# Batch 0 of a chunked-attention and sine-MLP kernel: loads by GpSimd with the cast, units of even and odd blocks, and other places for zeros and key transposes

## The chip, the cores and the metric

The kernel runs on one NeuronCore of a Trainium2 chip. Five engines work on it: TensorE (PE in the profile, with PEld for its weight loads), VectorE (DVE), ScalarE (ACT), GpSimd (POOL) and SyncE (SP, which here only issues DMAs). The metric is the device time of one execution in microseconds, the median of several runs.

## The reference

Two parts follow each other. The attention has 4 batches, 8 heads, 768 positions and 64 elements a head. The positions are cut into chunks of 32; a chunk sees 8 memory rows, and the keys from 16 before it to 8 behind it:

```
for c in range(nc):                      # 24 chunks
    k_full = concatenate([mem_k, k[l_start:r_end]])
    v_full = concatenate([mem_v, v[l_start:r_end]])
    a = softmax(scale * q_c @ k_full.T)
    out[c] = a @ v_full
```

The result, reshaped to 3072 tokens of 512 elements, goes through a feed-forward layer with a hidden width of 2048:

```
h = x @ w_in
s = sin(alpha * h)
g = h + s * s / alpha
out = g @ w_out
```

Inputs and output are float32; the kernel computes in bfloat16 with float32 accumulation.

## The kernel before

A batch's 768 positions are cut into 8 blocks of 96 (three chunks of 32). A block's window is 128 rows: 64 key rows from 16 ahead of the block, 8 memory rows, 56 more key rows. Keys and queries stand transposed in SBUF (`kT`, `qT`: head elements on partitions, two heads to one tile of 128), values stand by window rows (`vw`: 64 elements and a column of ones, which gives the softmax sum). What a chunk may not see is masked: in batch 0 by one more matmul (`mrow` against the indicator `mind`), in the others by a bias of the exponential (`biasm`).

The work is written out by hand as one list of words, `WORDS`, with one line per stage. Each word issues one step, and each engine and each DMA queue executes its steps in the order in which the words issue them. Stage 0 of the list (the first line) is the attention of batch 0; the next three lines hold the feed-forward of one batch beside the attention of the next; the last holds the feed-forward of batch 3. The words that matter here (a digit behind a letter is a head pair, a block or a tile; A, V or P names the engine, ACT, DVE or POOL):

- `dq`, `dk`, `V`: issue loads of q, k and v from POOL's queue, which casts to bfloat16 on the way (L190, L196). `dk068` is k of batch 0, heads 6 and 7.
- `a`: cast a float32 load of q or k to bfloat16 (L683). In the kernel before, head pairs 0 to 2 of batch 0's q and k come as float32 through SP and ACT (L756) and are cast by ACT and DVE.
- `k`, `l`: 12 transposes on PE of a head pair's k or q (L307); `K`, `L`: the copy from PSUM to `kT` or `qT`.
- `s`, `v`: scores with the exponential, and values with the division, of one unit (L347, L372). A unit of batch 0 is a head pair and a half of the blocks: blocks 0 to 3 (half 0) or 4 to 7 (half 1). In the other batches a unit is one block with all heads.
- `t`, `T`: turn a unit's result on PE and copy it to `xT` by DVE or ACT; `c`: the same by a DMA transpose from SP.
- `b`, `h`: feed-forward tile, the first and the second 384 columns (4 matmuls each), `h` followed by the sine on ACT; `q`: the square; `g`: DVE's last step, which fills `gT` and frees the tile's two PSUM banks. Four such pairs of banks exist.
- `o`, `f`: the second matrix product, fed in pieces between the other work; its result goes through one of three `o_sb` buffers to a store on SP.
- `R`, `X`: row loads of k and q of batches 2 and 3 from POOL, and their DMA transposes from SP into `kT` and `qT`.
- `I`, `U`: loads of `w_in` and `w_out` from POOL, by tiles (`I27` is tiles 2 to 6, `I7g` 7 to 15).
- `y`, `z`: matmuls on zeros, 128 or 512 columns each; `C`: constants and zeros; `W`: a table load on ACT.

Loads from POOL are issued by POOL itself, so its queue holds its memsets, copies and load issues in one order.

Of the kernel before, what the change touches and what calls it, by code (L numbers as in the profile page):

```python
# [9 lines left out]
P = 128  # L10
QW = 96
# [15 lines left out]
    ),  # L27
    (
# [5 lines left out]
    ),  # L34
    (
# [5 lines left out]
    ),  # L41
    (
# [5 lines left out]
    ),  # L48
    (
# [72 lines left out]
def kernel(  # L122
# [12 lines left out]
    nc = tc.nc  # L135
# [36 lines left out]
    pts = [consts.tile([P, H * QW + 32], BF, name=f"pt{i}") for i in range(NPT)]  # L172
# [6 lines left out]
    memk_bf = memv_st[0:NK, 0]  # L179
    memk_st = memv_st[96:104].rearrange("n b h d -> n b (h d)")  # L180
    memkT = consts.tile([P, HP, NK], BF, name="memkT")
# [36 lines left out]

    def win(vflat, row, n, height):
        a = vflat[row:row + 1, :]  # L220
        return bass.AP(tensor=a.tensor, offset=a.offset, ap=[[D, height], [QW * D, n], [1, D]])
# [20 lines left out]
    def put_memk(b):  # L242
        nc.vector.tensor_copy(
            kTs[b % 2][:, :, 24:856].rearrange("p g (j c) -> p g j c", c=104)[:, :, :, 40:40 + NM],
            memkT[:, :, NM * b:NM * b + NM].unsqueeze(2).to_broadcast([P, HP, NJ, NM]),
        )
# [289 lines left out]
    class Stage:  # L536
# [39 lines left out]
        def do_P(self, a):  # L576
            self.early(a, 1)
# [311 lines left out]
```

## Time and profile before

| | us |
|---|---|
| median of 3 runs | 215.34 (215.27 to 215.65) |
| profiled execution, its own time | 214.68 |
| span of that execution | 212.8 |
| PE busy | 204.9 (96%) |
| DVE busy | 139.9 (66%) |
| ACT busy | 143.7 (68%) |
| POOL busy | 100.9 (47%) |

The chain of work that ended last is 78% PE, 8% DVE, 5% ACT and 4% DMA; the DMA share is one float32 load of keys at the start (`kq_f<-in_k_dram`). A busy PE is not PE at its peak, since matmuls are pipelined and their ends are modelled; and in the opening PE is also busy with matmuls on zeros, which compute nothing. Times inside the profile count from the start of the span.

### The profile page before, as it was taken

The numbers are of one execution on the slowest core, as the hardware profiler recorded it, in microseconds if no ns is written. First come the engines' busy times: TensorE is split into PE (matmuls) and PEld (weight loads), VectorE is DVE, ScalarE is ACT, GpSimd is POOL, SyncE is SP. The second block draws the span as 40 slices with busy tenths as digits, with TensorE's granted clock in tenths as the row PEclk, the third lists the DMA queues.
The fourth block names the chain that finished last, engine by engine and source line by source line (L and its number), as shares of the span: only waits on it lengthen the run. The fifth ranks groups of instructions, "written<-read, shape, count | busy, mean of one in ns | idle before, by whom it ended". The sixth has DMA issues, their size and how long they took to land.

```text
span 212.8 us, 4568 instructions
## 1 busy us (share of the span) xinstructions
PE 204.9 (96%) x1772; PEld 118.1 (55%) x1772; DVE 139.9 (66%) x210; ACT 143.7 (68%) x229; POOL 100.9 (47%) x142
## 2 busy tenths in 40 slices
PE   7879999999999999999999999999999999999994
PEld 7456665565455556555455555554555555554453
DVE  4788788999452749976766649897247187865010
ACT  2579898978848469968837199887856189891110
POOL 8998605589697297109795048664000022200000
PEclk9999999999999999999999999999999999999999
DMA  5999999999999999999999259999944400000312
GB/s 156 332 158 139 212 207 204 205 139 183 131 160 155 176 114 129 121 144 146 146 152 183 74 125 125 137 157 133 134 104 107 137 0 0 3 2 0 148 52 99
DMA packets 95853, 27.82 MB, mean 131 GB/s; under 512 B 84808, under 2 KB 92376, under 8 KB 95832
## 3 DMA queue, kind: packets, MB, share of 16 engines
q0 software_dynamic: 69152, 13.64, 89.3%
q1 hardware_dynamic: 25720, 12.68, 29.6%
q10 hardware_dynamic: 960, 1.21, 1.7%
q8 instruction: 14, 0.23, 0.6%
q14 instruction: 7, 0.06, 0.1%
HBM read 29.66 MB, written 6.29 MB: 169 GB/s over the span
## 4 chain that ended last, share of the span: by engine, by line
PE 78%; DVE 8%; ACT 5%; DMA 4%; issue 3%; SPq 1%; DVEq 0%; ACTq 0%
PE ps L495 39%; PE ps L457 30%; DMA kq_f<-in_k_dram 4%; PE ps L447 3%; DVE gT L484 2%; PE ps L418 2%; DVE x_blk L387 2%; DVE s L480 2%; ACT s L477 2%; PE ps L399 1%; ACT pt L365 1%; PE ps L312 1%; ACT u L472 1%; DVE q_bf L686 1%; DVE rinv L386 0%
## 5 line engine op out<-in xcount | busy, mean ns | idle before, releaser
L495 PE MATMUL ps<-w_out_sb,gT 128*128 128x512 bf16 (+1 forms) x400 | 89.1, 371 | 0.0
L457 PE MATMUL ps<-xT,w_in_sb 128*128 128x384 bf16 x512 | 85.9, 326 | 0.6 <-DVE gT L484 0.4
L484 DVE SCALAR_TENSOR_TENSOR gT<-s,inv_alpha,ps 128x768 bf16<-128x768 f32 x64 | 63.1, 1012 | 12.3 <-ACT s L477 5.2
L457 PEld LDWEIGHTS <-w_in_sb 128*128 128x128 bf16 x512 | 49.7, 98 | 35.2 <-issue 2.0
L472 ACT ACTIVATE u<-ps,alpha_sb 128x768 f32<-128x768 f32 x64 | 56.6, 894 | 16.9 <-PE ps L457 14.4
L495 PEld LDWEIGHTS <-gT 128*128 128x128 bf16 x400 | 37.1, 98 | 37.1 <-DVE gT L484 0.2
L480 POOL TENSOR_TENSOR s<-u 128x768 f32<-128x768 f32 x11 | 17.2, 1568 | 67.2 <-ACT u L472 56.4
L432 ACT ACTIVATE pt<-ps,biasm 128x256 bf16<-128x256 f32 x72 | 27.1, 488 | 10.5 <-PE ps L418 10.5
L502 DVE COPY o_sb<-ps 128x512 f32<-128x512 f32 (+1 forms) x15 | 10.0, 669 | 27.6 <-PE ps L495 25.7
L480 DVE TENSOR_TENSOR s<-u 128x768 f32<-128x768 f32 x23 | 21.9, 953 | 7.6 <-ACT u L472 7.5
L477 ACT ACTIVATE s<-u 128x768 f32<-128x768 f32 x30 | 25.0, 841 | 0.5
L387 DVE TENSOR_TENSOR x_blk<-ps,rinv 96x512 bf16<-96x512 f32 x32 | 22.0, 687 | 1.1
L502 ACT COPY o_sb<-ps 128x512 f32<-128x512 f32 (+1 forms) x10 | 5.7, 572 | 22.0 <-PE ps L495 22.0
L208 POOL DMA_DIRECT2D vw<-in_v_dram x13 | 12.0, 926 | 6.3 <-PE ps L399 5.4
L386 DVE RECIPROCAL rinv<-ps 96x8 f32<-96x8 f32 x32 | 6.4, 199 | 13.1 <-PE ps L447 12.7
L215 POOL DMA_DIRECT2D vw<-in_v_dram x13 | 13.3, 1024 | 1.6 <-DMA vw<-in_v_dram 1.6
L274 POOL DMA_DIRECT2D kst<-in_k_dram x16 | 13.0, 815 | 1.8 <-DMA vw<-in_v_dram 1.2
L268 POOL DMA_DIRECT2D kst<-in_k_dram x16 | 11.1, 691 | 2.1 <-DMA kst<-in_k_dram 1.0
L281 POOL DMA_DIRECT2D q_bf<-in_q_dram x12 | 10.7, 911 | 0.0
L402 ACT COPY xT<-ps 128x384 bf16<-128x384 bf16 x10 | 5.0, 496 | 8.2 <-PE ps L399 8.2
L447 PEld LDWEIGHTS <-pt 128*128 128x128 bf16 x192 | 8.2, 97 | 4.2 <-ACT pt L432 0.3
L447 PE MATMUL ps<-vw,pt 128*128 128x65 bf16 x192 | 8.9, 193 | 0.0
(83 smaller groups left out, 140.7 us busy)
## 6 DMA issues: line engine op xcount, KB each, us to landing
out_dram<-o_sb SPq DMA_DIRECT2D x23, 256.0 KB, 2.2
q_bf<-in_q_dram POOLq DMA_DIRECT2D x12, 128.0 KB, 7.7
kq_f<-in_k_dram SPq DMA_DIRECT2D x3, 384.0 KB, 6.2
kq_f<-in_q_dram ACTq DMA_DIRECT2D x3, 384.0 KB, 7.9
w_in_sb<-in_moe_w_in_dram POOLq DMA_DIRECT2D x1, 1152.0 KB, 12.9
vw<-in_v_dram POOLq DMA_DIRECT2D x7, 128.0 KB, 7.7
vw<-in_v_dram POOLq DMA_DIRECT2D x8, 112.0 KB, 8.1
kst<-in_k_dram POOLq DMA_DIRECT2D x14, 64.0 KB, 5.5
```

The costliest lines, as they stand in the source:

```text
L215: nc.gpsimd.dma_start(vw[72:128, c0:hi, 0:D], win(vflat, base + QW * c0 + 48, hi - c0, 56))
L274: nc.gpsimd.dma_start(kst[72:72 + n, j, :].rearrange("p (h d) -> p h d", d=D), k[b, :, QW * j + 48:QW * j + 48 + n, :].rearrange("h p d -> ...
L387: nc.vector.tensor_tensor(out=x_blk[:].rearrange("p g e d -> p e g d"), in0=otv[0:QW, :, :, 0:D], in1=rinv[:].unsqueeze(3).to_broadcast([Q ...
L432: nc.scalar.activation(pt[:, 0:H * QW].rearrange("p (g e c) -> p g e c", g=2, e=4)[:, :, :, 32 * m:32 * m + 32], sc[:, :, 0:4 * QW].rearra ...
L447: nc.tensor.matmul(otv[:, e, hp, :], pt[:, QW * i:QW * i + P], vws[b % 2][:, 2 * hp + e, j, 0:D + 1],)
L457: nc.tensor.matmul(t["hT"][:, hf, 0:HALF], w_in_sb[:, kt, P * t["ft"]:P * t["ft"] + P], t["xT"][:, kt, HALF * hf:HALF * hf + HALF], start= ...
L472: nc.scalar.activation(t["u"][:], t["hT"][:, :, 0:HALF], ACTF.Sin, scale=alpha_sb[:, ft:ft + 1])
L477: nc.scalar.activation(s2[:], u[:], ACTF.Square)
L480: e.tensor_tensor(out=s2[:], in0=u[:], in1=u[:], op=ALU.mult)
L484: nc.vector.scalar_tensor_tensor(out=gT[:, ft, :].rearrange("p (e c) -> p e c", e=2), in0=t["s2"][:], scalar=inv_alpha[:, ft:ft + 1], in1= ...
L495: nc.tensor.matmul(o[:, c0:c1], gT[:, ft, P * s:P * s + P], w_out_sb[:, ft, c0:c1], start=(ft == 0), stop=(ft == FT - 1),)
L502: copier(state["engines"][state["o"] % len(state["engines"])])(o_sb[:, c0:c1], o[:, c0:c1])
```

## The change

It changes the first line of words and what it calls, and rewrites the order of the other lines.

1. Loads of batch 0. The float32 loads through SP and ACT and the six casts (`a`) go. All of q, k and v of batch 0 come from POOL's queue with the cast, by head pairs: q 0-1 is issued ahead of the identity, then k 0-1, k 2-3, k 4-5, q 2-3, v 0-1, q 4-5, k 6-7, v 2-3, q 6-7, v 4-5, and v 6-7 in four pieces of even and odd blocks (`G030`, `G031`). The loads of w_in 0 to 1 and 2 to 6 come behind them.
2. Units of batch 0 are the even and the odd blocks of a head pair instead of the first and the last four. Tiles 0 and 1 of batch 0's feed-forward are opened by the new word `j` on even columns, and these two are finished by two DVE instructions of 384 columns instead of one of 768.
3. Memory rows. mem_k is transposed in float32 and copied from PSUM straight to its places in both `kT`; mem_v of batch 0 is spread by head pairs from the float32 load (`n`, three on ACT, one on DVE) instead of a cast and one DVE copy.
4. Zeros and constants. Zeros of `pt`, of the first `kT` and of the first `vw` and its ones move from POOL to DVE, the sums behind `mind` to DVE and its copies to ACT; those of the second `kT` and `vw` stay on POOL and come later. Twelve matmuls on 512 columns of zeros take the place of the 40 on 128 columns at the start.
5. Batch 2. The new words `r` and `x` issue work of the batch after next: sixteen row loads (`r16`) and six key transposes (`x6`) stand in the second line of words; `x6` comes ahead of two stores.

The core of the diff, with the first line of words whole and of the second line the beginning and the end:

```diff
-        'y1 y1 y1 Ci y1 a4A We y1 Cb a1A y1 y2 y1 y1 dq068 Cl y1 Cm y1 Cf z1 z1 eVA z1 eVA a0A Ck m0 Cz z1 '
-        'dk068 Cp V024 z1 z1 V002 z1 a2V V068 z1 z1 Cv l0 z1 a5V z1 L0A k1 k0 z1 k2 l1 K1A V046 K0A a6V L1A '
-        's00 s10 s11 K2V l2 k3 L2V K3A s01 v11 dm l3 L3A v10 s20 v01 s30 v00 s31 v30 s21 v31 z1 T01 v20 T30 '
-        'I02 Cs T00 v21 t10 T20 t31 z1 t11 I27 t21 Ws '
+        'n0A Cb dk002 dk024 Ci Cz dk046 We Cd z1 z1 z1 z1 z1 z1 z1 z1 z1 z1 z1 z1 k0 z1 K0V Cm z1 Cp n1V l0 '
+        'z1 z1 dq024 k1 z1 V002 dq046 Ck K1A y1 L0A Cv l1 z1 s01 dk068 s00 L1V s10 v01 s11 z1 Cy v00 V024 '
+        'dq068 l2 z1 k2 n2A K2A n3A V046 L2V t00 G030 v10 t01 G031 s20 v11 l3 dm k3 L3A K3V s21 T11 v20 I02 '
+        's30 v21 s31 v30 Cs T10 v31 T20 T30 T21 T31 Cl Ws Cw I27 '
...
-        'o8 b0 h0 I7g q0V U69 U12 b1 h1 dq108 q1A b4 h4 b3 g0 h3 b6 g1 dk108 q4V g4 q3A b2 h2 h6 b5 h5 Ufg g3 '
+        'j0 j1 h0 I7g q0V h1 g0 q1V dk108 b4 h4 b3 U01 h3 U56 g1 q4V b6 b2 q3A o8 g4 h2 dq108 h6 g3 U45 U12 '
...
-        'g15 f7 h14 V125 k1 k0 g12 l1 K1V k3 L1V L3A q14V K3A K0A V102 dy f9 g14 s61 f16 m1 s70 s3 f13 v0 f3 '
-        'v6 Z2 c6 f6 v3 f5 s542 T3 f10 T0 v4 f6 v2 f2 v1 c4 c2 f7 v7 f1 T1 f3 v5 Ws T7 f8 t5 '
+        'b14 g15 f5 q12A h14 g12 f1 k1 k3 k0 l1 L3A f5 L1A K1V V102 f1 K3A K0V q14A g14 f3 m1 s61 f16 dy s073 '
+        'f14 v6 f5 v3 r16 Z2 c6 v0 f8 s542 f10 t3 v4 f7 v2 c2 T0 v1 c4 x6 f9 v7 We t1 f5 v5 We T7 f6 t5 '
...
+    def load_v_half(b, hp, half):
+        assert b < B - 1
+        vw = vws[b % 2][:].rearrange("p h j c -> p (h j) c")
+        vflat = v.rearrange("b h s d -> (b h s) d")
+        c0 = 2 * hp * NJ + half
...
+        for c, r0, r1 in ((lo, 0, 64), (c0, 72, 128)):
...
+            nc.gpsimd.dma_start(
+                vw[r0:r1, c:c1:2, 0:D],
...
+    def put_memv_first(hp, eng):
+        copier(eng)(
+            vws[0][64:72, 2 * hp:2 * hp + 2, :, 0:D],
+            memv_f[64:72, 2 * hp:2 * hp + 2].unsqueeze(2).to_broadcast([NM, 2, NJ, D]),
+        )
...
         for i in range(4):
-            j = 4 * half + i
+            j = 2 * i + half
...
+    def every_other(cols, half):
+        return cols.rearrange("p (a e c) -> p e a c", e=2, c=QW)[:, half]
...
     def finish(t, gT):
         ft = t["ft"]
+        if t["split"]:
+            for hf in range(2):
+                nc.vector.scalar_tensor_tensor(
+                    out=every_other(gT[:, ft, :], hf),
...
+        def do_j(self, a):
+            self.tile[int(a)] = opened(int(a), self.xT if self.i >= 0 else self.next_x(), True)
+            half_tile(self.tile[int(a)], 0)
...
+        def do_r(self, a):
+            for _ in range(int(a)):
+                self.next_rows()["R"].pop(0)()
+
+        def do_x(self, a):
+            for _ in range(int(a)):
+                self.next_rows()["X"].pop(0)()
...
-    for hp in range(HP - 1):
-        load_f(nc.sync, k, hp, kq_f[hp])
-        load_f(nc.scalar, q, hp, kq_f[4 + hp])
-        if hp == 0:
-            nc.sync.dma_start(memv_f[64:72], mem_v[0].rearrange("h n d -> n h d"))
+    nc.sync.dma_start(memv_f[64:72], mem_v[0].rearrange("h n d -> n h d"))
     nc.vector.memset(zeros[:], 0.0)
     nc.vector.memset(tiny[:], 0.0)
+    nc.vector.memset(ident[:], 0.0)
+    load_one(q, q_bf, 0, 0, 2)
+    masks.make_identity(nc, ident[:], nomemset=True)
     nc.vector.memset(mcol[:], 0.0)
-    masks.make_identity(nc, ident[:])
-    for vw in vws:
-        nc.gpsimd.memset(vw[0:32, 0, 0, 0:D], 0.0)
-        nc.gpsimd.memset(vw[96:128, H - 1, NJ - 1, 0:D], 0.0)
+    nc.vector.memset(vws[0][0:32, 0, 0, 0:D], 0.0)
...
     def const_k():
-        nc.vector.tensor_copy(memk_bf, memk_f[0:NK])
...
+                mt[:, g, :], memk_f[0:NK, 2 * g:2 * g + 2, :].rearrange("p e d -> p (e d)"),
+                ident_f[0:NK, 0:NK]
...
     def const_v():
-        for vw in vws:
-            nc.gpsimd.memset(vw[:, :, :, D:D + 1], 1.0)
+        nc.vector.memset(vws[0][:, :, :, D:D + 1], 1.0)
+
+    def const_w():
+        nc.gpsimd.memset(vws[1][:, :, :, D:D + 1], 1.0)
+        nc.gpsimd.memset(vws[1][96:128, H - 1, NJ - 1, 0:D], 0.0)
```

More of the change, by code (lines that the diff above doesn't have):

```diff
@@ L171 @@
     NPT = 8
-    pts = [consts.tile([P, H * QW + 32], BF, name=f"pt{i}") for i in range(NPT)]
+    pt_all = consts.tile([P, NPT, H * QW + 32], BF, name="pt")
+    pts = [pt_all[:, i] for i in range(NPT)]
     memv_st = consts.tile([P, B, H, D], BF, name="memv_st")
@@ L462, in half_tile, with opened @@
             )
-    def opened(ft, xT):
+    def opened(ft, xT, split=False):
         hT, bs = banks.pair()
-        return {"ft": ft, "xT": xT, "hT": hT, "bs": bs, "from": [0, 0]}
+        return {"ft": ft, "xT": xT, "hT": hT, "bs": bs, "from": [0, 0], "split": split}
     def sine(t):
@@ L532 @@
     feed = Feed()
+    ahead = {}
     kq = (k_bf, q_bf)
@@ L550, in __init__ @@
             if 1 <= i + 1 < B:
-                self.queue = {"R": row_loads(i + 1), "X": crosses(i + 1)}
+                self.queue = ahead.pop(i + 1, None) or self.row_work(i + 1)
         def next_x(self):
@@ L675, in do_m, with do_n, do_G @@
             put_memv(int(a))
+        def do_n(self, a):
+            put_memv_first(int(a[0]), a[1])
+        def do_G(self, a):
+            load_v_half(*(int(c) for c in a))
         def do_H(self, a):
@@ L725, in do_y, with row_work, next_rows @@
                 nc.tensor.matmul(ps[:, b, c:c + P], zeros[:, 0:P], zeros[:, c:c + P])
+        def row_work(self, b):
+            return {"R": row_loads(b), "X": crosses(b)}
+        def next_rows(self):
+            b = self.b + 1
+            if b not in ahead:
+                ahead[b] = self.row_work(b)
+            return ahead[b]
+        def do_r(self, a):
[4 more added lines that the diff above has]
+                self.next_rows()["X"].pop(0)()
         def do_R(self, a):
@@ L738, in warm @@
         nc.scalar.activation(tiny[:], zeros[0:1, 0:1], func)
-    kq_f = [mlp.tile([P, 2, 6 * D], F32, name="kq_f", tag=t) for t in ("u", "s2") * 4]
     memk_f = mlp.tile([P, H, D], F32, name="memk_f", tag="o_sb", bufs=3)
```

91 lines of the change are left out of this document (45 added, 46 removed), and 29 rows, old and new, of the table WORDS.

## The prediction

> **What bounds the kernel now.** I read the table of windows first, then the chain of work that ended last, then the timeline of the opening, the loads with their landing times, and the groups of instructions of two stretches. The windows, cut where the chain changes its nature (columns: stretch, its length, then busy time and count of PE, PEld, DVE, ACT, POOL, granted clock, DMA share, GB/s):
>
> ```profile
> 0.00:24.78 24.78, 20.51 (x340) 15.44 (x341) 19.23 (x49) 16.21 (x24) 22.33 (x52) 1.00 1.68 198
> 24.78:35.41 10.63, 10.57 (x69) 6.26 (x66) 8.35 (x11) 9.13 (x12) 1.98 (x2) 1.00 1.20 207
> 35.41:75.10 39.69, 39.57 (x405) 22.43 (x405) 27.00 (x38) 29.02 (x52) 28.80 (x37) 1.00 1.80 164
> 75.10:209.75 134.65, 134.22 (x964) 73.94 (x962) 85.27 (x113) 89.02 (x144) 47.80 (x53) 1.00 0.98 104
> ```
>
> From 35.41 to 209.75 PE is idle for 0.12 + 0.43 = 0.55 us in all. Nothing that the change reorders there can win more than about half a microsecond. What can be won lies in the first stretch: 24.78 us of batch 0's attention, in which PE's 20.51 busy us are partly matmuls on zeros. The chain (start, length, what), and the opening's timeline (start, length, engine, line, operation, count):
>
> ```profile
> 2.57 8.45 DMA kq_f<-in_k_dram
> ...
> 14.60 2.22 ACT pt L365 x3
> ...
> 24.95 2.62 PE ps L457 x16
> ```
>
> ```profile
> 1.20 4.45 PE L725 MATMUL ps<-zeros 128*128 128x128 bf16 x40 [1.20 <-DVE tiny L762]
> 6.37 0.81 PE L719 MATMUL ps<-zeros 128*128 128x512 bf16 x3
> 6.40 0.83 ACT L686 CAST q_bf<-kq_f 128x768 bf16<-128x768 f32 x1 [1.95 <-DMA kq_f<-in_q_dram]
> 9.69 0.53 PE L312 MATMUL ps<-ident,q_bf 128*64 128x128 bf16 x12
> 11.25 1.50 ACT L323 COPY kT<-ps 128x768 bf16<-128x768 bf16 x2 [0.20 <-PE ps L312]
> 18.82 2.41 ACT L365 ACTIVATE pt<-ps 128x768 bf16<-128x768 f32 x3
> 22.14 1.48 ACT L402 COPY xT<-ps 128x384 bf16<-128x384 bf16 x3
> 24.64 1.28 ACT L738 ACT_TABLE_LOAD   x1
> 24.78 17.40 PE L457 MATMUL ps<-xT,w_in_sb 128*128 128x384 bf16 x104
> 26.28 0.90 ACT L472 ACTIVATE u<-ps,alpha_sb 128x768 f32<-128x768 f32 x1
> ```
>
> The reader is to see three dates: the third float load of keys lands at 11.02 (2.57 + 8.45), the first exponentials start at 14.60, the first feed-forward matmul at 24.78. From there the chain is PE, with one stretch in which ACT and DVE lead.
>
> **The change part by part.** *Start of the exponentials.* The six float loads and their six casts go; the same data comes through GpSimd's queue, cast on the way. The rows of that queue (KB, us from issue to landing; then two issues on POOL):
>
> ```profile
> q_bf<-in_q_dram POOLq DMA_DIRECT2D x1, 192.0 KB, 7.8
> k_bf<-in_k_dram POOLq DMA_DIRECT2D x1, 192.0 KB, 7.7
> vw<-in_v_dram POOLq DMA_DIRECT2D x1, 64.0 KB, 2.6
> w_in_sb<-in_moe_w_in_dram POOLq DMA_DIRECT2D x1, 640.0 KB, 8.1
> q_bf<-in_q_dram POOLq DMA_DIRECT2D x1, 768.0 KB, 16.5
> k_bf<-in_k_dram POOLq DMA_DIRECT2D x1, 768.0 KB, 19.5
> 21.25 0.89 POOL L191 DMA_DIRECT2D q_bf<-in_q_dram  x1 [0.78 <-ACT pt L365]
> 22.13 0.89 POOL L191 DMA_DIRECT2D k_bf<-in_k_dram  x1
> ```
>
> The last two land at 37.75 and 41.63, so the queue delivers 768 KB in 3.9 us, 198 KB a us. A pair of heads (192 KB) costs 1.0 us once data flows. The time to the first data is the open price: 2.6 us for 64 KB on an idle queue, or 7.7 us for 192 KB beside the float loads. I take the low end, 2.6 + 128/198 = 3.3 us, because the float traffic that stood beside the 7.7 is what the change removes, and I keep 7.7 for the range. The first load is issued at about 0.75 and the second, keys of heads 0 and 1, at about 2.0; that one lands at 5.3. PE cannot use it yet: its twelve matmuls on zeros are 6144 columns, of which the first 5120 cost 4.45 us from 1.20 and the last two 0.27 each, to 6.2. Then come three turns of 0.53, four more zeros and a small transpose of about 0.25 each: 6.2 + 1.6 + 1.25 = 9.1. ACT copies keys and queries (0.75 each back to back, the first 0.8) to 10.65, and the first exponential starts at about 11.0 against 14.60: 3.6 us earlier. In this sum the load has 0.9 us of cover; beyond that each microsecond costs one.
>
> The Trainium skill, page "DMA: Bandwidth & Descriptors", section on the anatomy of a SWDGE DMA, gives a fixed 2.0 us plus bytes over 436 GB/s, an estimate of 2.9 us for this pair. By that the second load lands at 4.9 and the start stays at 11.0; by the 7.7 row it would be 14.5.
>
> *From the first exponential to the last copy into xT, on ACT.* Before, from 14.60 to the table load at 24.64, 10.0 us. After, in the written order: 8 exponentials at 0.77 (6.2, mean of the two rows of three), a key and a query copy (1.5), two of the new spreads of mem_v (n2, n3), each 1024 elements on 8 partitions, 1.05 by the cast row's 0.83 for 768, and six xT copies at 0.49 (2.95): 12.75, to 23.75. Six xT copies where there were four, and the two spreads, are most of the difference. DVE is not later: eight pairs of
>
> ```profile
> L387 DVE TENSOR_TENSOR x_blk<-ps,rinv 96x512 bf16<-96x512 f32 x8 | 5.5, 687 | 0.3
> L386 DVE RECIPROCAL rinv<-ps 96x8 f32<-96x8 f32 x8 | 1.6, 198 | 0.4 <-PE ps L377 0.4
> ```
>
> are 7.1 us and about 2.5 of copies stand between them, from 12.2 to 21.8. Units of even and odd blocks change no count of matmuls. They let the two new opening words (j0, j1) run on even columns while ACT still copies the last two odd ones, so PE starts 1.0 before ACT ends, at about 22.7 instead of 24.78: 2.1 us.
>
> *What is given back at once.* The sine's table load waits for ACT: 23.75 + 1.28 + 0.2 = 25.2, so the first sine gains only 26.28 - 25.2 = 1.1. In 24.78 to 35.41 ACT is busy 9.13 and DVE 8.35 of 10.63 us; the chain there runs over them. Two further costs fall on DVE: square 1 moves to it and the two split tiles are finished in two halves.
>
> ```profile
> L480 DVE TENSOR_TENSOR s<-u 128x768 f32<-128x768 f32 x3 | 2.9, 954 | 1.8 <-ACT u L472 1.8
> ```
>
> That is 0.95 plus perhaps 0.15 a split tile, 1.25 in all; ACT loses 0.85. Of the 2.1 us I take 1.2 as what arrives at the PE-bound part: the sine's 1.1 is the low bound if ACT and DVE lead throughout, 2.1 the high one if they never do.
>
> *GpSimd's queue, and w_in behind it.* Feed-forward tile 4 is the third and needs w_in 2 to 6, issued last. Issue times on POOL, and one issue that met a DVE copy:
>
> ```profile
> L191 POOL DMA_DIRECT2D k_bf<-in_k_dram x2 | 1.6, 812 | 0.0
> L208 POOL DMA_DIRECT2D vw<-in_v_dram x4 | 3.6, 907 | 0.0
> L847 POOL MEMSET kst<- 32x512 bf16 x1 | 0.6, 564 | 0.0
> L844 POOL MEMSET vw<- 128x64 bf16 x2 | 1.0, 804 | 0.0
> 73.33 0.69 POOL L208 DMA_DIRECT2D vw<-in_v_dram  x1 [5.38 <-PE ps L399]
> 9.19 1.83 POOL L215 DMA_DIRECT2D vw<-in_v_dram  x1
> 9.36 1.22 DVE L224 COPY vw<-memv_st 8x4096 bf16<-8x4096 bf16 x1
> ```
>
> From 0.75: eight pair loads at 0.81 (6.5), six V pieces at 0.91 (5.4), four half pieces at 0.69 (2.8), three small ones at 0.7 (2.1), the memsets left on POOL (2.3), identity 0.3: its issue is at about 20.2. It lands 2.6 + 576/198 = 5.5 later at best, 8.1 by its own row: 25.7 to 28.3. PE wants it after 16 matmuls of 17.40/104 = 0.167, at 22.7 + 2.7 = 25.4. I take 25.7, nearest to the idle queue, since six memsets stand just ahead of it; the 0.3 lies inside the ACT and DVE lead. Before, the same point was 24.78 + 2.7 = 27.5.
>
> *At nothing:* the mem_k transposes in float, the zeros and mind moved to DVE and ACT (both wait for loads until about 6), the removed 1.22 copy. If that cover goes, they cost up to 1 us. *Batch 2:* the sixteen row loads keep their place on POOL; six key transposes move ahead of two stores on SP.
>
> ```profile
> 72.22 3.69 SPq L505 DMA_DIRECT2D out_dram<-o_sb  x2
> 76.09 9.87 SPq L296 DMA_TRANSPOSE kT<-kst  x6
> ```
>
> The stores go some 10 us later, to about 82; the third output buffer is free, and the feed of the next output tiles only begins near 91, so this is hidden. Without that cover it costs PE up to 9.9. The six transposes wait for their row loads, and behind them on SP wait those stores and then the query transposes, which move up by the same six. The later words are reordered with the same counts: 0.3 either way.
>
> Sum: 214.68 for the profiled execution (span 212.8 and 1.9 around it) less 1.2 is 213.5; the median of the three runs, 215.34, stands 0.66 higher, so 214.1.
>
> **The rivals.** *Late first data (slower).* Keys 0 and 1 take 7.7 us as their rows do and land at 9.7, 3.5 after PE is ready. The feed-forward starts at 26.2, net 1.2 - 3.5: 2.3 us slower, 217.6; with a landing at 8.0, 1.8 late, 215.9. It decides from a landing at 7.4 (6.2 + 1.2). For it: every 192 KB row. Against: the float loads beside them, and the 2.6.
>
> *w_in late (slower).* POOL's issues stretch, or the piece takes its 8.1: at 28.3 PE stands 0.8 behind the old kernel's 27.5, 216.1. It decides at 27.5. For it: the issue of 1.83 under a DVE copy of 1.22, against 0.91; two such meetings make 22.0 of 20.2. Against: the DVE copies and casts of that form mostly go. The Trainium skill, page "SBUF — State Buffer", section on the two separate sides, says that DVE in a two-port mode locks GpSimd out of the descriptor ring and that loads from ACT or SP are immune; by it this change moves six loads into the exposed queue. The 1.83 agrees.
>
> *All given back (no change).* ACT and DVE lead from 25 to 35 and the extra 1.25 on DVE eats the sine's 1.1: 215.3.
>
> **How the numbers follow.** Forecast 0.6, of its own 213.1 to 214.9; given back 0.13; late first data 0.16; late w_in 0.11. Nothing under 0.2% (0.43 us) can be told from no change, which gives faster 0.6, same 0.13, slower 0.27. The range runs from 212.9 (2.1 kept and 0.3 from the later words) to 216.2, past the late w_in and a landing at 8.0.
>
> **What would show it.** Right: first exponential near 11, PE on zeros until 6.2 with the keys there before, last xT copy near 23.7 with ACT without gaps, first feed-forward matmul near 22.7, and every later boundary earlier by about the same. Wrong: PE waiting for k_bf or q_bf, PE waiting for w_in after 25, gaps on PE between 25 and 36 that were not there, stores waiting behind the transposes after 75.

## The result, and the profile after

The change made the kernel 1.6% slower. Six runs of the changed kernel have a median of 218.69 us (217.71 to 219.19), six of the kernel before 215.31 (214.7 to 215.65): a ratio of 1.0164, 95% interval 1.0138 to 1.0191. The profiled execution took 219.17 us, its span is 217.4; before, 214.68 and 212.8. The spans differ by 4.6, the medians by 3.4; what follows divides up the 4.6. Of e13, e15, e16 and e18 below, one execution each was over 1.5% above the fastest; it stands in the medians shown and is left out of the ratios.

The windows of the changed kernel, cut at the first feed-forward matmul of each stage (columns as in the prediction):

```profile
0.00:25.80 25.80, 21.19 (x303) 13.14 (x303) 15.29 (x51) 16.73 (x26) 22.94 (x39) 0.93 1.36 134
25.80:77.48 51.68, 50.17 (x469) 28.50 (x469) 34.16 (x50) 38.32 (x63) 30.70 (x38) 1.00 1.57 169
77.48:124.42 46.94, 46.78 (x376) 25.89 (x374) 34.18 (x49) 34.95 (x58) 34.08 (x44) 1.00 1.65 147
124.42:171.75 47.33, 46.19 (x357) 24.95 (x355) 30.03 (x43) 32.92 (x55) 8.82 (x7) 1.00 0.88 115
171.75:217.40 45.65, 42.04 (x241) 23.28 (x239) 23.15 (x25) 20.62 (x26) 7.33 (x5) 0.99 0.13 47
```

The same cuts of the kernel before (its first, to 24.78, is in the prediction):

```profile
24.78:74.94 50.16, 49.98 (x473) 28.60 (x471) 35.35 (x49) 38.01 (x62) 30.62 (x38) 1.00 1.67 174
74.94:121.52 46.58, 46.56 (x377) 25.69 (x374) 33.49 (x48) 32.58 (x57) 27.62 (x36) 1.00 1.59 137
121.52:167.58 46.06, 45.90 (x356) 25.02 (x354) 30.03 (x42) 34.02 (x57) 15.88 (x14) 1.00 1.15 123
167.58:212.80 45.22, 41.91 (x241) 23.32 (x239) 21.75 (x24) 22.92 (x30) 4.46 (x3) 1.00 0.13 47
```

The bill is the difference of the lengths: opening +1.02, stage 0 +1.52, stage 1 +0.36, stage 2 +1.27, last stage +0.43, together 4.60. No stretch gained. In stage 0 PE's busy time grew by 0.19 only, so 1.33 of its 1.52 is idle PE; in stage 2, 0.98 of its 1.27 is idle PE. The last 0.43 lies behind the last copy of an output tile: 2.7 us from its end to the span's end before, 3.1 after.

The opening, on PE and then on ACT:

```profile
6.49 0.53 PE L335 MATMUL ps<-ident,k_bf 128*64 128x128 bf16 x12 [0.87 <-DMA k_bf<-in_k_dram]
...
11.65 0.85 PE L335 MATMUL ps<-ident,q_bf 128*64 128x128 bf16 x12 [1.60 <-DMA q_bf<-in_q_dram]
```

```profile
13.84 2.92 ACT L388 ACTIVATE pt<-ps 128x768 bf16<-128x768 f32 x4 [3.24 <-PE ps L381]
...
26.24 1.28 ACT L796 ACT_TABLE_LOAD   x1
...
27.96 1.70 ACT L500 ACTIVATE u<-ps,alpha_sb 128x768 f32<-128x768 f32 x2 [0.22 <-PE ps L484]
```

The chain of work that ended last has one piece of 6.94 us there, the fifth pair load (queries 2 and 3, issued at 4.67), and the turn behind it:

```profile
4.67 6.94 DMA q_bf<-in_q_dram
11.61 0.04 issue
11.65 0.85 PE ps L335 x12
```

PE's order puts the turn of queries 2 and 3 (l1) ahead of the first scores of heads 0 and 1, whose own loads have long landed. So the first exponential comes at 13.84, not at 11.0. (Other profiles of the same opening wait less here; they are set side by side behind e12.) The turn took 0.85 us where the one at 6.49 took 0.53: PE's clock was at half speed for some 3.4 us.

The early stretch of stage 0, with PE idle for 0.86 and 0.38 us:

```profile
25.80 6.02 PE L484 MATMUL ps<-xT,w_in_sb 128*128 128x384 bf16 x36
32.68 2.12 PE L484 MATMUL ps<-xT,w_in_sb 128*128 128x384 bf16 x12 [0.86 <-DVE gT L514]
35.18 2.76 PE L484 MATMUL ps<-xT,w_in_sb 128*128 128x384 bf16 x16 [0.38 <-DVE gT L522]
```

And the chain over the first of those waits:

```profile
28.89 0.97 DVE s L508
29.91 0.05 issue
29.96 1.14 DVE gT L514 x2
31.11 0.88 DVE s L508
32.01 1.14 DVE gT L514 x2
33.15 0.88 DVE s L508
```

DVE works without a gap from 28.89 on: square, split finish, square, split finish, square. The first eight tiles, 10.63 us before (24.78 to 35.41), take 12.30 (25.80 to 38.10).

The start of stage 2, and what POOL and SP did just before it:

```profile
124.42 1.47 PE L484 MATMUL ps<-xT,w_in_sb 128*128 128x384 bf16 x8
...
126.49 5.37 PE L484 MATMUL ps<-xT,w_in_sb 128*128 128x384 bf16 x32 [0.60 <-DMA xT<-x_blk]
```

```profile
118.26 5.28 POOL L304 DMA_DIRECT2D q_bf<-in_q_dram  x6
```

```profile
121.22 5.14 DMA xT<-x_blk
```

The last row is a piece of the chain: PE, after eight matmuls, needs a block that a DMA transpose is still bringing, 5.14 us after its issue. In the kernel before, the same six query loads stood behind a square on POOL and started 8.70 us later, when the transposes were done, and PE began stage 2 without a wait:

```profile
121.52 13.39 PE L457 MATMUL ps<-xT,w_in_sb 128*128 128x384 bf16 x80
...
125.55 1.46 POOL L480 TENSOR_TENSOR s<-u 128x768 f32<-128x768 f32 x1 [10.65 <-issue]
126.96 5.33 POOL L281 DMA_DIRECT2D q_bf<-in_q_dram  x6
```

### The profile page after: what moved, and what is told of

Its sections match the earlier page's. It is cut to its first block, busy times and chain, and to the rows that moved or that the text cites. A ratio compares the mean times of both kernels' runs of the same rounds, so it can differ in the third digit from the quotient of the medians.

```text
span 217.4 us, 4471 instructions
## 1 busy us (share of the span) xinstructions
PE 206.4 (95%) x1734; PEld 115.8 (53%) x1734; DVE 136.8 (63%) x217; ACT 143.5 (66%) x227; POOL 103.9 (48%) x131
## 4 chain that ended last, share of the span: by engine, by line
PE 68%; DVE 13%; DMA 6%; ACT 5%; issue 5%; POOL 2%; DVEq 0%; POOLq 0%; ACTq 0%
PE ps L533 36%; PE ps L484 23%; DVE gT L522 5%; DVE s L508 4%; DMA q_bf<-in_q_dram 3%; PE ps L444 2%; DMA xT<-x_blk 2%; PE ps L473 2%; ACT u L500 2%; DVE x_blk L410 2%; PE ps L335 1%; DVE gT L514 1%; POOL k_bf L189 1%; ACT qT L355 1%; PE ps L373 1%
## 5 line engine op out<-in xcount | busy, mean ns | idle before, releaser
L484 PE MATMUL ps<-xT,w_in_sb 128*128 128x384 bf16 x512 | 86.9, 326 | 2.9 <-DVE gT L522 1.0
L522 DVE SCALAR_TENSOR_TENSOR gT<-s,inv_alpha,ps 128x768 bf16<-128x768 f32 x62 | 61.0, 1012 | 13.0 <-ACT s L505 7.6
L508 POOL TENSOR_TENSOR s<-u 128x768 f32<-128x768 f32 x12 | 18.9, 1584 | 67.2 <-ACT u L500 67.2
L508 DVE TENSOR_TENSOR s<-u 128x768 f32<-128x768 f32 x24 | 23.1, 961 | 10.4 <-ACT u L500 10.3
L505 ACT ACTIVATE s<-u 128x768 f32<-128x768 f32 x28 | 23.5, 842 | 0.7
L206 POOL DMA_DIRECT2D vw<-in_v_dram x12 | 11.1, 926 | 7.1 <-PE ps L422 7.1
L213 POOL DMA_DIRECT2D vw<-in_v_dram x12 | 11.6, 967 | 0.5 <-DMA k_bf<-in_k_dram 0.5
L278 POOL DMA_DIRECT2D w_out_sb<-in_moe_w_out_dram x10 | 6.4, 651 | 6.2 <-DMA w_in_sb<-in_moe_w_in_dram 6.2
```

The costliest lines, as they stand in the source:

```text
L213: nc.gpsimd.dma_start(vw[72:128, c0:hi, 0:D], win(vflat, base + QW * c0 + 48, hi - c0, 56))
L484: nc.tensor.matmul(h.rearrange("p (a c) -> p a c", c=QW) if t["split"] else h, w_in_sb[:, kt, P * t["ft"]:P * t["ft"] + P], every_other(t[ ...
L505: nc.scalar.activation(s2[:], u[:], ACTF.Square)
L508: e.tensor_tensor(out=s2[:], in0=u[:], in1=u[:], op=ALU.mult)
L522: nc.vector.scalar_tensor_tensor(out=gT[:, ft, :].rearrange("p (e c) -> p e c", e=2), in0=t["s2"][:], scalar=inv_alpha[:, ft:ft + 1], in1= ...
```

## The experiments

Ratios are against the kernel before, run on the same chip in the same job. The medians of the kernel before in the five jobs are 214.51, 214.49, 214.27, 214.73 and 214.47. In the expectations, "the kernel before" and "the changed kernel" are the two given ones.

### Which lines cost: e1 and e2

e1 is the changed kernel with its first line of words and the four later lines of the kernel before. e2 is the converse: the kernel before with its own first line, the new units (even and odd blocks) and the four new later lines.

```
e1: WORDS = (after[0], before[1], before[2], before[3], before[4])
e2: WORDS = (before[0], after[1], after[2], after[3], after[4])
```

> The changed kernel's first line of words (its loads, constants, units, mem spreads) with the old kernel's other four lines. Theory 'opening': the loss is made in the opening, because q of heads 2 and 3, the fifth load, lands at 11.6 and stands in PE's order ahead of the first scores; then this kernel keeps most of it, 2 to 3 us slower than before, 217.3 to 218.3. Rival 'later lines': the opening costs only the 1.0 us by which the first feed-forward matmul is later (25.80 against 24.78), the rest comes from the reordered lines; then 216.0 to 216.5.

> The old kernel's opening (float loads through SP and ACT, casts, its constants) with units of even and odd blocks and the changed kernel's other four lines, j0 and j1 and the row loads and key transposes ahead of the stores among them. Theory 'opening': within 0.5 us of before, 214.8 to 215.8, and first feed-forward matmul near 24.8. Rival 'later lines': 1.5 to 2.5 us slower than before, 216.8 to 217.8, with PE waiting behind DVE in the first eight tiles and for the DMA transposes into xT near 122.

e1: 217.43 us, ratio 1.0113 (1.0050 to 1.0177). e2: 218.79, ratio 1.0188 (1.0119 to 1.0257). Stage by stage, from the timelines (us from one first feed-forward matmul to the next):

| | first feed-forward | stage 0 | stage 1 | stage 2 | last stage |
|---|---|---|---|---|---|
| before | 24.78 | 50.16 | 46.58 | 46.06 | 45.22 |
| after | 25.80 | 51.68 | 46.94 | 47.33 | 45.65 |
| e1 | 26.80 | 50.17 | 46.59 | 46.07 | 45.57 |
| e2 | 24.16 | 51.68 | 47.22 | 47.73 | 46.01 |

The lengths of stages 0 to 2 go with their lines of words, to 0.01 us in e1. So the new lines cost by themselves and not as a result of the opening, and the new opening costs by itself too. The last 0.4 comes with e1 as well, whose last line is the old one; no experiment looked for it. e1's time lies where the theory 'opening' had it, but e2 is slower than both theories said, so both parts cost. The two ratios do not add up to that of the change: e2 meets a second wait for the transposes (1.02 us at the start of stage 2 and 0.60 in the last stage), e1 a worse opening.

### The opening's loads: e3, e4, e12

e3 loads four heads of queries in the first load instead of two; e4 puts the turn of queries 2 and 3 behind the first scores; e12 exchanges two loads.

```
e3: -load_one(q, q_bf, 0, 0, 2)   +load_one(q, q_bf, 0, 0, 4)
    -dk002 dk024 ... dq024         +dk004 ...
e4: -Cv l1 z1 s01 dk068 s00 L1V    +Cv z1 s01 dk068 s00 l1 L1V
e12: -dk046 We ... dq024 k1        +dq024 We ... dk046 k1
```

> The changed kernel with one load of q for heads 0 to 3 and one of k for heads 0 to 3 in place of two each; k 4-5 third. Theory 'fifth load': q and k of heads 0 to 3 are then the first two loads, land by about 8.5, the first exponential starts near 11 instead of 13.84, and the total falls by 1.5 to 2.5 us against the changed kernel, to 216.2 to 217.2. Rival 'the queue delivers some 115 KB a us at this stage, whatever the piece': the second load lands near 9.5 to 10, the first exponential near 12.5, and the total falls by about 1.

> The changed kernel with the turn of q of heads 2 and 3 (l1) moved behind the first two score units in PE's order; loads unchanged. Theory 'fifth load in PE's order': the first exponential starts near 11.3 instead of 13.84, two of the sixteen ACT steps run in the gap, and the total falls by 1 to 1.5 us, to 217.2 to 217.7. Rival 'the load itself': the third exponential still waits for q 2-3 and everything behind it keeps its date; the total falls by less than 0.5.

> The changed kernel with two loads of the opening exchanged: queries 2 and 3 ahead of keys 4 and 5; l1 stays ahead of the first scores. Theory A (192 KB loads land one after another, 1.2 to 2.5 us apart, so a load's place in the queue sets its landing): queries 2 and 3 land near 10.2 instead of 11.6, PE's wait of 1.6 us for them shrinks to 0 to 0.4, the first exponential at 12.2 to 12.8 instead of 13.8. Rival B (what holds the load is something else than its place, such as one slow engine of it): it lands at 11 or later. For the end I expect 0.3 to 1.2 us less by theory A.

e3: 220.55 us, ratio 1.0261 (1.0204 to 1.0319). A longer first load holds the first turn back, PE waits 2.46 us for keys and the first exponential comes at 14.69: not the hoped-for gain. e4: 219.29, ratio 1.0229 (1.0156 to 1.0301). Its opening, on ACT and PE:

```profile
11.87 1.51 ACT L388 ACTIVATE pt<-ps 128x768 bf16<-128x768 f32 x2 [0.43 <-PE ps L381]
...
25.14 1.28 ACT L796 ACT_TABLE_LOAD   x1
```

```profile
13.67 0.35 PE L381 MATMUL ps<-qT,kT 64*128 64x96 bf16 x8 [0.79 <-DVE qT L355]
...
24.70 5.55 PE L484 MATMUL ps<-xT,w_in_sb 128*128 128x384 bf16 x32
```

In these two profiles the exponentials start 2.0 us earlier, and the first feed-forward matmul comes 1.1 earlier than in the changed kernel: no better than 24.78. The total gained nothing. e12: 219.23, ratio 1.0247 (1.0183 to 1.0311). PE no longer waits for queries 2 and 3, but it waited 1.87 us for the first keys, ran at half clock behind that, and the first exponential stayed at 13.80.

How far one profile can be trusted here is seen in the six that have the changed kernel's first line word for word:

| | after | e1 | e5 | e6 | e7 | e16 |
|---|---|---|---|---|---|---|
| PE's wait for queries 2 and 3 | 1.60 | none | 0.34 | 1.24 | none | 0.50 |
| first exponential | 13.84 | 11.96 | 12.24 | 13.45 | 12.09 | 12.33 |
| first feed-forward | 25.80 | 26.80 | 25.74 | 25.95 | 25.23 | 26.82 |

So the long wait for the fifth load is no fixed property of the order: without it (e1, e7) the exponentials start near 12 with l1 where it was, and the feed-forward starts at 26.80 and 25.23, on either side of 25.80. That e4's edit gained the 2.0 us is therefore not shown. With the old first line the feed-forward began at 24.78 and 23.98 (e8), so in the mean the new opening costs 1.7 us (26.06 against 24.38), rather than the 1.02 of one pair of profiles, and differences of less than about a microsecond between single openings say little.

### Stage 0 and stage 2: e5, e6, e7, e16, e8

e5 restores the first eight words of stage 0, e6 one letter of batch 2's line, e7 both; e16 restores the eight words but leaves square 1 on DVE. e8 is the kernel before with the converse of e6's letter.

```
e5:  -j0 j1 h0 I7g q0V h1 g0 q1V    +b0 h0 I7g q0V b1 h1 g0 q1A
e6:  -b1 q5A q3V h1                 +b1 q5A q3P h1
e16: -j0 j1 h0 I7g q0V h1 g0 q1V    +b0 h0 I7g q0V b1 h1 g0 q1V
e8:  -q0V g0 q3P R6                 +q0V g0 q3V R6     (kernel before)
```

> The changed kernel with the first eight words of stage 0's line as they were: both tiles opened whole (b0, b1, no split and no finishing in two halves) and square 1 back on ACT. Theory A (the new start of stage 0 costs the 1.5 us by which the first eight tiles grew from 10.6 to 12.3): the first eight tiles take 10.5 to 11.0 us again, the two waits for gT of 0.86 and 0.38 shrink, the time falls by 1.0 to 1.6 us against the changed kernel. Rival B (the 1.5 is the opening's late end, weights and copies that are not ready, and follows wherever PE starts): the eight tiles stay at 12 us and the time does not move by more than 0.4.

> The changed kernel with one letter of batch 2's line changed: square 3 on GpSimd as before, ahead of the six query loads of R6, instead of on DVE. Theory A (with no square ahead of them the six loads start at 118 instead of 127 us and run beside the transposes into xT, which then take 5.1 us and stop PE at the start of stage 2): the loads are issued near 126, PE's wait for xT of 0.6 goes, and stage 2 falls from 47.3 to between 46.1 and 46.8, the time by 0.5 to 1.2. Rival B (the wait for xT is the lateness of the transposes themselves, or of their place on SP): the loads move and the wait stays; the time is the same within 0.3.

> The changed kernel with both edits: the old first eight words of stage 0 and square 3 of batch 2's line on GpSimd. Theory A: the two gains add up to 1.5 to 2.8 us, which leaves the kernel 0.5 to 2 us above the one before, by the opening. Rival B: not more than the better of the two alone.

> The changed kernel with the first two tiles of stage 0 opened whole (b0, b1, no finish in two halves), and square 1 left on DVE. Theory A (the square on DVE, 0.95 us, is the greater half, as in the prediction's sum): stage 0 falls by 0.2 to 0.6 us of the 1.4 that putting both back won. Rival B (the split finish, two instructions of 1.14 that wait for each other and for PE, is the greater half): stage 0 falls by 0.8 to 1.4 us.

> The kernel before with the converse of one letter: square 3 of batch 2's line on DVE instead of GpSimd, so that the six query loads have nothing ahead of them. Theory A: the loads are issued some 5 to 8 us earlier, PE waits for the transposes into xT for 0.4 to 1.3 us at the start of stage 2, and the time rises by 0.4 to 1.3. Rival B (the order of the words in the changed kernel is to blame, not the loads): no wait for xT, the time is the same within 0.3.

| | us | ratio | stage 0 | stage 2 |
|---|---|---|---|---|
| after | | 1.0164 (1.0138 to 1.0191) | 51.68 | 47.33 |
| e5 | 217.68 | 1.0120 (1.0057 to 1.0182) | 50.65 | 47.43 |
| e6 | 218.15 | 1.0150 (1.0094 to 1.0206) | 51.68 | 46.54 |
| e7 | 217.17 | 1.0102 (1.0053 to 1.0151) | 50.31 | 46.54 |
| e16 | 219.32 | 1.0199 (1.0130 to 1.0269) | 51.16 | 47.97 |
| e8 | 216.61 | 1.0098 (1.0063 to 1.0132) | 50.16 | 47.44 |

The intervals of the first five overlap, so the verdict rests on the stage lengths. e5 takes 1.03 off stage 0 and nothing else; with e7's 1.37 that is theory A. The first eight tiles take 10.72 in both. With the changed kernel's line the stage took 51.68 or 51.69 in six profiles and 52.13 in e4; with e5's start it took 50.11 to 50.80 in four (e5, e7, e9, e10), so the start costs 0.9 to 1.6. e16 splits it: opening the tiles whole is worth 0.52, within A's range, and the step from e16 to e5, square 1 back on ACT, another 0.51; by the four profiles that second part is 0.36 to 1.05. Both parts are real; which is the greater is not shown. In e5 the early stretch is one run of 72 matmuls:

```profile
25.74 12.18 PE L484 MATMUL ps<-xT,w_in_sb 128*128 128x384 bf16 x72
...
38.33 5.36 PE L484 MATMUL ps<-xT,w_in_sb 128*128 128x384 bf16 x32 [0.41 <-DVE gT L522]
```

e6 takes 0.79 off stage 2 and touches nothing else; the loads start late again and the wait for xT is gone:

```profile
128.56 1.46 POOL L508 TENSOR_TENSOR s<-u 128x768 f32<-128x768 f32 x1 [9.80 <-ACT u L500]
129.98 5.33 POOL L304 DMA_DIRECT2D q_bf<-in_q_dram  x6
```

```profile
124.56 6.67 PE L484 MATMUL ps<-xT,w_in_sb 128*128 128x384 bf16 x40
...
131.54 13.77 PE L484 MATMUL ps<-xT,w_in_sb 128*128 128x384 bf16 x80 [0.30 <-DVE gT L522]
```

The other profiles bear this out. In all eleven with the square on POOL ahead of the loads PE does not wait for xT at the start of stage 2, which takes 46.06 to 46.08 us with the old line and 46.54 or 46.55 with e6's. In all eight with the changed kernel's line PE waits there, from 0.25 us (e14) to 1.31 (e3), and the stage less this wait takes 46.7 in each. So the wait is the greater part of e6's 0.79 (0.60, with 0.2 for the rest), and the remaining 0.48 against the kernel before belongs to the order of other words, which no experiment took apart.

e8 is the converse: one letter makes the kernel before 2.1 us slower by medians (214.49 to 216.61), more than theory A's 1.3. In the profiled run stage 2 is longer by 1.38; there the six query loads are issued from 113.57 on, and PE meets two waits, one behind the other:

```profile
123.13 5.42 PE L457 MATMUL ps<-xT,w_in_sb 128*128 128x384 bf16 x32 [0.75 <-ACT tiny L738]
129.08 13.49 PE L457 MATMUL ps<-xT,w_in_sb 128*128 128x384 bf16 x80 [0.52 <-DVE gT L484]
```

The first is named after a small instruction of ACT; but the last transpose into xT was issued at 117.7 and the transposes of that stretch landed 5.0 to 5.3 us after issue, which is 122.7 to 123.0, so I take it for the same wait as in the changed kernel. The second is for a finish on DVE, where the square now stands as well; in the kernel before that wait was 0.16. The letter brings both: 0.75 us of the profiled run go by the first and 0.52 by the second.

### What ends the opening: e9, e10, e11, e13, e14, e15, e17, e18

These start from the changed kernel's opening. e9 joins e4 and e7. e10 is e9 with the two spreads of mem_v (n2, n3) on DVE. e11 has that opening ahead of the old later lines, e13 and e15 are e11 with one load moved, or two left out. e14 fills the changed kernel's wait with matmuls on zeros. e17 and e18 take the spreads out of the exponentials' stretch.

```
e9:  e4 + e7
e10: -n2A K2A n3A                   +n2V K2A n3V          (on e9)
e11: e10's first line, later lines of before
e13: -s01 dk068 s00 ... v00 V024    +s01 s00 ... v00 V024 dk068   (on e11)
e14: -Cv l1                         +Cv z1 z1 z1 z1 z1 z1 l1
e15: +if b == 0 and h0 == 6: nc.gpsimd.memset(dst[:, h0:h1], 0.0); return   (load_one, on e11)
e17: -z1 k0 ... n2V K2A n3V         +z1 n2A n3A k0 ... K2A        (on e13)
e18: -dk046 ... dq024, s01 s00 l1   +dq024 ... dk046, s01 l1 s00  (on e17)
```

> The changed kernel with the old first eight words of stage 0, square 3 of batch 2's line on GpSimd, and the turn of queries 2 and 3 (l1) behind the first scores in the opening. Theory A (each of the three is worth what its trace showed: 1.4, 0.8 and 0.5 to 1.1): the first exponential at 11.9, the first feed-forward matmul at 24.2 to 24.8, 2.0 to 3.0 us below the changed kernel, that is between 0.3 above and 0.6 below the time with the other two alone less 0.6. Rival B (the opening's start does not carry to the end, as when l1 alone was moved): no more than 0.2 below the kernel with the other two put back.

> The same and the two spreads of mem_v that stand between the exponentials of the opening (n2 and n3, 1.04 us each on ACT) on DVE. Theory A (the opening is a row of ACT instructions from the first exponential to the table load, as the sum of 12.75 us in the prediction had it, so that what comes off ACT comes off the opening): the table load 1.2 to 2.0 us earlier, the first feed-forward matmul at 22.8 to 23.8, the time 0.7 to 1.5 lower than without. Rival B (V's pieces or DVE end the opening; DVE gets 1.4 us more): the first feed-forward matmul within 0.3 of the other kernel's, and the waits for V or for x_blk grow by about 1.0.

> The new opening with l1 behind the first scores and n2 and n3 on DVE, and all later lines as in the kernel before. Theory A: with the first feed-forward matmul at 22.8 to 23.8 against 24.2 to 24.8 and the later stages 183.9 us from the first feed-forward matmul to the median's end as before, the time is 0.4 to 1.5 us below the kernel before. Rival B (the opening through the GpSimd queue ends at 24.7 or later whatever the order): the time is 0 to 1.5 us above the kernel before.

> As e11 (new opening with l1 behind the first scores and the spreads on DVE, old later lines), with the load of keys 6 and 7 moved behind V of heads 2 and 3. Theory A (the queue hands over its loads one after another, so that a load's place sets its landing): V of heads 2 and 3 lands 1.0 to 1.6 us earlier, PE's wait of 1.6 for it falls to 0 to 0.6, the first feed-forward matmul comes at 24.6 to 25.6 instead of 26.6, unless keys 6 and 7 are then waited for. Rival B (the wait ends by something else, such as POOL's issue time): V lands where it did, the wait stays above 1.2.

> The changed kernel with six more matmuls on zeros (0.22 us each, 1.3 in all) ahead of l1 in the opening, where PE waited 1.6 us for queries 2 and 3. Theory A (the 3.4 us at half clock after that wait cost time, and come only from PE's idle stretch): clock 0.998 or more in every run, the first exponential 0.4 to 0.9 us earlier than 13.84, the time 0.3 to 1.0 lower than the changed kernel and more even. Rival B (the half clock falls into slack): the clock is back to 1.0 and the first feed-forward matmul stays within 0.3 of 25.8.

> As e11, with the loads of keys 6, 7 and queries 6, 7 of batch 0 replaced by a memset of the same tiles on GpSimd (384 KB less in the queue; heads 6 and 7 of batch 0 are computed from zeros). Theory A (the queue's bytes are the limit of the opening): V's wait of 1.6 us goes, nothing waits for a DMA after the first exponential, the first feed-forward matmul at 23.0 to 24.5. Rival B (ACT, DVE and PE among themselves set the opening's end): within 0.5 of 26.6 less the wait, that is 24.6 to 25.5.

> As e13 (new opening, l1 behind the first scores, keys 6 and 7 behind V of heads 2 and 3, old later lines), with the two spreads n2 and n3 on ACT ahead of the first turn of keys, where ACT stood idle from 5.8 to 9.3. Theory A (the opening from the first exponential on is a row of ACT and DVE work, and the two spreads, 2.1 us, are what it has more than the old one): from the first exponential to the first feed-forward matmul 10.8 to 12.0 us instead of 12.8 with the spreads on ACT and 16.0 on DVE, that matmul at 22.3 to 23.7, and the time 0.5 to 2.0 us below the kernel before. Rival B (a wait for V or for keys takes its place): the first feed-forward matmul at 24.3 or later, a wait for a DMA of over 1 us on PE, the time 0 to 2 above the kernel before.

> As e17, with queries 2 and 3 ahead of keys 4 and 5 in the queue and their turn between the first two scores. Theory A: within 0.5 us of e17, on either side; the fourth pair of scores starts 0.3 to 0.5 us earlier, and nothing waits for keys 4 and 5. Rival B: as of e17.

| | us | ratio | first exponential | first feed-forward | what PE waited for in between |
|---|---|---|---|---|---|
| e9 | 217.62 | 1.0145 (1.0090 to 1.0199) | 11.53 | 25.20 | V 1.1, qT 0.8 |
| e10 | 217.87 | 1.0167 (1.0125 to 1.0208) | 11.28 | 26.61 | V 1.6, qT 0.8 |
| e11 | 217.18 | 1.0135 (1.0111 to 1.0160) | 11.20 | 26.57 | V 1.6, qT 0.8 |
| e13 | 218.30 | 1.0138 (1.0063 to 1.0214) | 11.22 | 27.24 | qT 1.3 and 0.8 |
| e14 | 219.24 | 1.0207 (1.0162 to 1.0251) | 15.64 | 27.60 | only small ones |
| e15 | 216.69 | 1.0097 (1.0063 to 1.0131) | 11.77 | 27.05 | qT 1.5 and 0.8 |
| e17 | 216.26 | 1.0082 (1.0052 to 1.0111) | 11.47 | 25.06 | qT 0.8, queries 0.7, V 0.4 |
| e18 | 217.22 | 1.0100 (1.0060 to 1.0141) | | | |

Theory A failed in all of them at the end of the opening or in the time, and the rivals' dates did not always hold either (e10, e11 and e15 ended later than both said): a wait that is taken away is followed by the next. e18's profiled execution ran at half clock for 6.8 us from 23.04 on, so its dates are not set beside the others; its time is 217.22 us against e17's 216.26, with intervals that overlap. In e11 it is V, in e13 V has landed and PE waits for a copy of queries, because the spreads now stand on DVE ahead of it:

```profile
PE ps L401 <- DMA vw<-in_v_dram: 1.6, 1, 1.6
```

```profile
PE ps L374 <- DVE qT L356: 1.3, 1, 1.3
```

The first row is of e11, the second of e13; columns are total, times, longest. In e13 keys 6 and 7 landed at 17.36 instead of 14.53, so a load's place does set its landing; V's second piece landed at 16.83 instead of 17.71, and PE's wait for it fell from 1.6 to 0.2 us, but with the old place it landed anywhere from 16.39 (e4) to 18.05 (e5). The end of the opening gained nothing. e15, with 384 KB less in the queue, loses V's wait too, meets the same one on DVE and ends at 27.05: the loads' bytes alone are not the limit. e14 says nothing on the clock: in its profile PE waited 2.26 us for the first keys and fell to half clock there, and its three runs at full clock took 218.5 to 219.4, no less than the changed kernel. e17, free of the spreads, has the lowest time with the new opening and is still 0.8% above the kernel before:

```profile
18.62 0.53 PE L336 MATMUL ps<-ident,q_bf 128*64 128x128 bf16 x12 [0.68 <-DMA q_bf<-in_q_dram]
...
20.59 0.42 PE L401 MATMUL ps<-vw,pt 128*128 128x65 bf16 x8 [0.40 <-DMA vw<-in_v_dram]
...
25.06 17.72 PE L485 MATMUL ps<-xT,w_in_sb 128*128 128x384 bf16 x104
```

From its first exponential 13.6 us pass, not the 10.8 to 12.0 I expected. Its feed-forward starts only 0.28 later than in the kernel before; 1.28 of the 1.9 by which its span is longer lie in stage 0 (51.44 us), whose words are the old ones: behind the first eight tiles PE is idle for 1.34 us there against 0.12, of which 0.46 are a wait for batch 1's keys. Why is open. None of the 16 profiles of the new opening (e18's left out) brought the first feed-forward matmul before 24.70 (24.70 to 27.60), though first exponentials ranged from 11.20 to 15.64; with the old opening it came at 23.98, 24.16 and 24.78. The DMA traffic from 5 to 10 us, in the kernel before and in the changed one, shows what both orders live on:

```profile
DMA packets 1222, 1.67 MB, mean 335 GB/s; under 512 B 55, under 2 KB 1222, under 8 KB 1222
q10 hardware_dynamic: 552, 0.80, 47.4%
q1 hardware_dynamic: 516, 0.75, 45.0%
q0 software_dynamic: 154, 0.12, 15.0%
```

```profile
DMA packets 1407, 0.75 MB, mean 150 GB/s; under 512 B 503, under 2 KB 1407, under 8 KB 1407
q0 software_dynamic: 1407, 0.75, 119.7%
```

The old opening had three queues at work and moved 1.67 MB, of which the 1.55 on q10 and q1 are float32, worth 0.78 in bfloat16: 0.90 MB of useful data, against 0.75 through GpSimd's queue alone. Whether some order of this queue ends the opening before 24 stays open: none of those tried did, and no single wait was found that decides it.

## Why the prediction was wrong, by its own steps

The forecast put the span 1.2 us below the kernel before; it came out 4.6 above. Of these 5.8 us, 3.1 are the opening (the first feed-forward matmul at 25.80, not 22.7), 0.6 stage 0 (1.52 lost, not 0.9) and 2.1 the later lines and the end (0.36, 1.27 and 0.43, not nothing).

*Start of the exponentials, failed, and the opening with it is the largest part.* The sum looked at the second load only. Keys 0 and 1 were used at 6.49 against the 6.2 reckoned, so that step was near; but it counted three turns ahead of the first scores, and the written order has four: the last is that of queries 2 and 3, the fifth load. The rate was wrong as well: 198 KB a us, taken from the last two landings of a backlog of 768 KB loads; here the first pair load took 3.6 us from its issue at 1.26,

```profile
q_bf<-in_q_dram POOLq DMA_DIRECT2D x1, 192.0 KB, 3.6
```

to 4.9, and the fifth landed at 11.61, so four of them took 1.7 us each, 114 KB a us (with pieces of V under way beside them). The first exponential came 2.8 later than forecast, and 1.0 to 2.5 later in the five other profiles with this first line.

*The rival of late first data, partly real.* Against 7.7, the profiled first keys came at 6.5. But over the 15 other profiles with this opening they were used between 6.66 and 8.39 (e3, with a load of twice the size, at 8.39; e14 at 8.05), so the point of 7.4 from which that rival decides was passed in three. The Trainium skill, page "DMA: Bandwidth & Descriptors", section on the anatomy of a SWDGE DMA, which I had weighed against this, made 2.9 us of a pair as an estimate (by the 384 KB of its float32 source); the trace has 3.9 from the issue of keys 0 and 1, at 2.52, to their landing.

*From the first exponential to the last copy, right in this profile by luck.* 13.84 to 26.24, the table load, is 12.4 us against 12.75. The same 12.40 stands in e3, e12 and e14, where the exponentials also start at 13.80 or later. Where they start earlier, 12.9 to 16.5 us pass, with PE waiting for V or for copies of queries in between. So the row of ACT instructions set the length only where it began late, and an early start did not carry to the end: the sum let every later load be there in time, and in the runs it was not. What ends the opening when it starts early stays open. PE also started 0.44 us ahead of ACT's end, not 1.0.

*What is given back at once, mis-sized.* I took 0.9 of 2.1 for the lead of ACT and DVE; the stretch of eight tiles grew by 1.67 (10.63 to 12.30). The two costs named, square 1 on DVE and the split of the first two tiles, were the right ones (0.51 and 0.52 in e5 and e16), and the two halves of a finish took 1.14 us against 1.01 for a whole one, near the 0.15 more that was taken; but they were charged against a slack on DVE that was not there: DVE is gapless from 28.89.

*w_in late, hidden by the late opening.* It landed at 27.11, not at 25.7. PE, which wanted it 2.7 us behind its start, at 28.5, did not wait; on the date of the forecast, 25.4, it would have, had the load landed at 27.11 all the same. It was waited for in e9 (0.52 us) and e17 (0.15).

*Batch 2's rows and stores, right.* The stores went at 83.65 (about 82 was forecast) and nothing waited for them.

*"The later words are reordered with the same counts: 0.3 either way", failed.* Stages 1 and 2 and the end cost 0.4, 1.3 and 0.4 us. Each of the four lines still has 16 squares, but not the same on each engine: eleven of them change theirs. One, square 3 of batch 2's line, went from POOL to DVE, and it had been holding back the six query loads behind it in POOL's order. Taking it away let them start at 118 instead of 127, beside the transposes that feed the next stage; it is 0.8 of the 1.3 (e6). The rest, and the 0.4 of stage 1, stay open. The prediction asked of moved steps what stands behind them; it did not ask that of a word that changes its engine.

## What to carry to other kernels

Read an engine's order word by word to the first instruction that waits for a load: an early start is worth what the latest load ahead of it allows, and what the loads behind it allow in turn. A step that leaves an in-order queue releases what stood behind it; look where those DMAs will now run, and for what else is in flight there. Where each of several removed waits is followed by another, compare the rate of supply over the stretch before you move single steps, and compare dates only with the spread that repeats of the same order show.

## What the runs showed of the hardware

PE's clock fell to half after idle stretches much shorter than I had thought. In the changed kernel PE idled 1.60 us, and the clock of the next stretch was

```profile
10.00:15.00 5.00, 3.40 (x46) 2.16 (x46) 1.59 (x4) 1.76 (x3) 4.13 (x7) 0.66 1.81 161
```

which is 3.4 us at half speed. The same followed idle stretches of 1.24 us (e6) to 2.46 (e3) in ten more profiles, but none followed 1.80 us in e5, 1.57 in e1, 1.45 in e9 or 1.41 in e16, and e18 fell to half clock behind stretches of 0.8 us at most: the length of one idle stretch alone does not decide it. The Trainium skill, page "TensorE: Matmul & The Clock Gate", section "Why this matters for your kernels", allows idle gaps up to about 3 us between bursts of matmuls; these traces show the fall behind gaps of less than half of that. A cost of it in the time is not seen: the changed kernel's one execution with it took 219.17 us, the five others 217.71 to 219.19.

The transposes from `x_blk` into `xT` took very different times from issue to landing, where the profile gives the landing. In the kernel before, the one issued at 110.00, while row loads of batch 3 were still landing, took 6.84 us, and the one at 118.32, behind them, 2.28. In the changed kernel the one at 116.48, between the row loads and the six query loads, took 2.42, and the one that PE waited for, beside the six, 5.14. In e8 one took 5.04 beside row loads and one 5.33 beside the six. All these loads come from GpSimd's queue, with the cast. That the loads are the cause rests on this and on e6 and the other profiles with the loads held back, where the wait is gone; how they slow a transpose is not shown.
